# Loading x for a fused attention and gated-MLP kernel: all tiles by DMA transposes from the first issue, the second half of w_in on one queue

## The chip, the cores and the metric

The kernel runs on one core of a Trainium2 chip. The metric is the device time of one execution in microseconds (us). A profile's span, from the first to the last instruction, is about 1.7 us shorter than that time (before: 207.5 us of span, 209.19 us of time in the same execution). Times of the kernel before spread over about 1 us, and a finding at the end shows what may make most of that.

## The reference

```python
x = A_x                                             # [1, 2048, 512] bf16
g = sigmoid((x * gate_w).sum(-1, keepdims=True))
a = hedgehog_linear_attention(x, wqkv, w_phi, wo)   # 32 heads of 16
z = gelu(x @ w_in)                                  # [2048, 1376]
z1 = z[..., :688]
z2 = layernorm(z[..., 688:])
b = (z1 * (w_sp @ z2 + b_sp)) @ w_out
return g * a + (1 - g) * b
```

The argument touches only the first step: `z2 = x @ w_in[:, 688:]`, for which x must lie transposed in SBUF.

## The kernel before

x has 16 tiles of 128 rows. In the kernel before, tiles 0 to 3 come by plain loads (`xs`) and TensorE (PE) transposes them; tiles 4 to 7 come by one DMA transpose each, tiles 8 to 15 by two of four tiles. The second half of w_in, `w_z2`, comes in four pieces of 172 KB (one for each 128 rows of the contraction, `dt`), three on ScalarE's queue and one on SyncE's. PE runs warm-up matmuls while it waits for the first data. One extra column of `w_z2` holds the gate vector: `gate_T` puts it there through PE and VectorE, and the second half (`j = 1`) of each z2 tile needs it.

```python
nc.sync.dma_start(out=xs[:, 0, :], in_=x2[0:P, :])
load_z2w(nc.scalar, 0)                      # w_z2 piece 0
nc.sync.dma_start(out=xs[:, 1, :], in_=x2[P:2 * P, :])
load_z2w(nc.scalar, 1)
load_z2w(nc.sync, 2)
nc.scalar.dma_start(out=gaterow[0:NDT, :], in_=gate_w.rearrange(...))
load_z2w(nc.scalar, 3)
nc.sync.dma_start(out=xs[:, 2:4, :], in_=...)          # tiles 2 and 3
for h in range(2):
    nc.sync.dma_start(out=w_z1[:, 2 * h:2 * h + 2, :], in_=...)
for i in range(4, 8):
    nc.sync.dma_start_transpose(out=xT[:, :, i * P:(i + 1) * P], in_=x2[i * P:(i + 1) * P, :])
# ... (cut)

def z2_first_two():
    # ... (cut)
    warm_up(6)                              # 128x512 matmuls on constants
    warm_up(5, P)                           # 128x128
    x_T(0, 0, 1, ...)                       # PE transposes of tile 0, copy to xT
    x_T(0, 1, NDT, ..., on_act=True)
    warm_up(3, P)
    one(0, 0, 0)                            # tile 0, dt 0, half 0
    # ... (tiles 0 and 1 interleaved, gate_T among them, transposes of 2 and 3; cut)

with tc.manual_schedule(engines={PE, Activation}):
    z2_first_two()
    z2_tile(2)
    z2_tile(3)
    b_T()                                   # a tiny matmul; then z1 begins
    # ... (cut)
```

The softmax here doesn't subtract the row's maximum and nothing guards it: scores larger than these inputs give would overflow.

## Time and profile before

| | before |
|---|---|
| time, median of the first 3 runs | 208.36 us (208.36 to 209.25) |
| span of the profiled run | 207.5 us |
| PE busy | 203.6 us, 98% |
| start of z1 (just after `b_T`) | 11.35 us |

Two lines of the page of before: the busy time of PE, and the chain that ended last by engine.

```profile
PE 203.6 (98%) x1456; PEld 122.5 (59%) x1456; DVE 131.4 (63%) x282; ACT 75.4 (36%) x122; POOL 46.6 (22%) x78
...
PE 98%; DVE 0%; issue 0%
```

PE bounds the kernel. Its first microseconds are another matter. The next lines are the chain of waits of before in order of time (start, length in us, what; L226 is the warm-up, L284 a transpose of x, L195 a matmul of z2 or z1, L294 the gate, L299 `b_T`).

```profile
0.84 3.25 PE zp L226 x11
4.10 0.43 PE pq L284 x4
...
4.84 0.29 PE zp L195
...
6.06 0.57 PE zp L195 x2
6.63 0.01 PE pq L294
6.64 1.34 PE zp L195 x8
...
9.01 2.34 PE zp L195 x16
11.35 0.01 PE pq L299
11.35 14.03 PE zp L195 x96
```

Read the length of one matmul from them: 0.57/2 = 0.29 us at 6.06, 2.34/16 = 0.146 us from 9.01 on. The array clock doubles in between; the trace's record of the granted clock has its first entry, full speed, at 6.70 us. (Before its first entry this record counts as 1.00 in the views, so the "PEclk" column says nothing of the first microseconds; the length of the matmuls does.) From 9.01 us on PE never waits again.

The DMA engines in that stretch of before: each line has a window in us, its length, PE's busy time and instructions, the granted clock, the mean busy share of the 16 DMA engines and the GB/s that they moved. A share above 1 means that packets overlap within an engine.

```profile
4.00:5.00 1.00, 1.00 (x10) 1.00 1.04 329
5.00:6.00 1.00, 1.00 (x9) 1.00 1.05 374
6.00:7.00 1.00, 1.00 (x7) 1.00 1.09 344
7.00:8.00 1.00, 1.00 (x11) 1.00 1.18 331
```

A load's landing is the time at which its last bytes have arrived. By its DMA issues the plain loads of tiles 0 and 1 landed about 3 us after their issue, the pieces of w_in 3.1 to 3.9 us after theirs (tile, queue, number of loads, size of one, median us from issue to landing):

```profile
xs<-in_A_x_dram SPq DMA_DIRECT2D x2, 128.0 KB, 3.1
w_z<-in_B_w_in_dram ACTq DMA_DIRECT2D x3, 172.0 KB, 3.5
```

### The profile page before, as it was taken

The numbers are of one execution on the slowest core, as the hardware profiler recorded it, in microseconds if no ns is written. First come the engines' busy times: TensorE is split into PE (matmuls) and PEld (weight loads), VectorE is DVE, ScalarE is ACT, GpSimd is POOL, SyncE is SP. The second block draws the span as 40 slices with busy tenths as digits, with TensorE's granted clock in tenths as the row PEclk, the third lists the DMA queues.
The fourth block names the chain that finished last, engine by engine and source line by source line (L and its number), as shares of the span: only waits on it lengthen the run. The fifth ranks groups of instructions, "written<-read, shape, count | busy, mean of one in ns | idle before, by whom it ended". The sixth has DMA issues, their size and how long they took to land.

```text
span 207.5 us, 3776 instructions
## 1 busy us (share of the span) xinstructions
PE 203.6 (98%) x1456; PEld 122.5 (59%) x1456; DVE 131.4 (63%) x282; ACT 75.4 (36%) x122; POOL 46.6 (22%) x78
## 2 busy tenths in 40 slices
PE   8999999999999999999999999999999999999994
PEld 4666666765566555556565666555455555665642
DVE  2477786764977777879797788555466563633330
ACT  3665666666422232333323033222251126002322
POOL 7020202020542227243342422222204220200000
PEclk9999999999999999999999999999999999999999
DMA  6999999999922014971403236753564469253442
GB/s 189 263 187 202 242 290 218 267 284 179 290 38 43 0 38 89 254 179 33 92 18 71 50 41 115 144 106 70 108 160 89 76 114 182 56 104 65 132 89 77
DMA packets 88970, 27.20 MB, mean 131 GB/s; under 512 B 82968, under 2 KB 88952, under 8 KB 88952
## 3 DMA queue, kind: packets, MB, share of 16 engines
q1 hardware_dynamic: 86176, 24.37, 59.1%
q10 hardware_dynamic: 2744, 2.60, 4.3%
q8 instruction: 11, 0.18, 0.4%
q14 instruction: 7, 0.06, 0.1%
q0 software_dynamic: 32, 0.00, 0.0%
HBM read 4.41 MB, written 2.10 MB: 31 GB/s over the span
## 4 chain that ended last, share of the span: by engine, by line
PE 98%; DVE 0%; issue 0%
PE mm L457 36%; PE zp L195 18%; PE mm L366 13%; PE mm L496 8%; PE mm L494 7%; PE mm L406 7%; PE at L470 2%; PE kvacc L422 2%; PE zp L226 2%; PE mm L499 1%; PE pq L319 1%; PE pq L284 1%; DVE ob L506 0%; PE pq L305 0%; PE tp L284 0%
## 5 line engine op out<-in xcount | busy, mean ns | idle before, releaser
L457 PE MATMUL mm<-z2all,wspT 128*128 128x344 bf16 x512 | 79.9, 309 | 0.0
L457 PEld LDWEIGHTS <-wspT 128*128 128x128 bf16 x512 | 49.0, 98 | 25.7 <-issue 0.4
L195 PE MATMUL zp<-w_z,xT 128*128 128x344 bf16 (+1 forms) x256 | 40.6, 312 | 0.0
L370 ACT ACTIVATE eq<-mm 128x512 bf16<-128x512 f32 x32 | 17.4, 594 | 51.3 <-POOL eq L383 21.5
L374 DVE TENSOR_REDUCE zs<-eq 128x64 f32<-128x1024 bf16 x16 | 19.5, 1220 | 20.3 <-ACT eq L370 20.3
L195 PEld LDWEIGHTS <-xT 128*128 128x128 bf16 x256 | 24.7, 99 | 11.2
L462 DVE SCALAR_TENSOR_TENSOR ucat<-mm,bT,z1all 128x344 bf16<-128x344 f32 x32 | 17.4, 544 | 21.8 <-PE mm L457 21.8
L383 POOL TENSOR_TENSOR eq<-eq,ratio 128x512 bf16<-128x512 bf16 x16 | 16.9, 1058 | 50.2 <-DVE ratio L382 41.7
L370 ACT ACTIVATE ek<-mm 128x512 bf16<-128x512 f32 x32 | 17.3, 600 | 27.1 <-PE mm L366 27.1
L510 ACT ACTIVATE ob<-mm,g_inv 128x512 bf16<-128x512 f32 (+1 forms) x16 | 10.9, 681 | 32.8 <-PE mm L499 28.3
L374 DVE TENSOR_REDUCE zs<-ek 128x64 f32<-128x1024 bf16 x16 | 19.3, 1209 | 2.8 <-ACT ek L370 2.8
L496 PE MATMUL mm<-wspT,uT 128*128 128x512 bf16 (+2 forms) x85 | 20.1, 366 | 0.0
L366 PEld LDWEIGHTS <-xT 128*128 128x128 bf16 x128 | 12.2, 98 | 12.9 <-PE mm L499 0.8
L383 POOL TENSOR_TENSOR ek<-ek,ratio 128x512 bf16<-128x512 bf16 x16 | 16.9, 1059 | 2.0 <-DVE ratio L382 1.2
L494 PE MATMUL mm<-wspT,oT 128*128 128x512 bf16 (+2 forms) x68 | 16.6, 366 | 0.0
L366 PE MATMUL mm<-wq_p,xT 128*128 128x512 bf16 x64 | 16.4, 379 | 0.0
L406 PE MATMUL mm<-wv_sb,xT 128*128 128x512 bf16 x64 | 16.4, 379 | 0.0
L366 PE MATMUL mm<-wk_p,xT 128*128 128x512 bf16 x64 | 16.3, 379 | 0.0
L213 DVE BATCH_NORM_STATS2 bn<-z2all 128x6 f32<-128x344 bf16 x32 | 14.9, 502 | 0.0
L210 ACT ACTIVATE z2all<-zp 128x688 bf16<-128x688 f32 x16 | 11.8, 744 | 7.3 <-PE zp L195 6.8
L264 ACT ACTIVATE z1all<-zp 128x688 bf16<-128x688 f32 x16 | 11.9, 744 | 6.7 <-PE zp L195 6.7
L496 PEld LDWEIGHTS <-uT 128*128 128x128 bf16 x85 | 8.1, 98 | 9.2
(79 smaller groups left out, 150.9 us busy)
## 6 DMA issues: line engine op xcount, KB each, us to landing
out_dram<-ob ACTq DMA_DIRECT2D x15, 128.0 KB, 1.8
wspT<-in_B_w_out_dram SPq DMA_DIRECT2D x2, 640.0 KB, 5.6
w_z<-in_B_w_in_dram SPq DMA_DIRECT2D x2, 344.0 KB, 4.2
w_z<-in_B_w_in_dram ACTq DMA_DIRECT2D x3, 172.0 KB, 3.5
wv_sb<-in_A_wqkv_dram SPq DMA_DIRECT2D x1, 512.0 KB, 4.7
wspT<-in_A_wo_dram SPq DMA_DIRECT2D x1, 512.0 KB, 6.2
xs<-in_A_x_dram SPq DMA_DIRECT2D x2, 128.0 KB, 3.1
xs<-in_A_x_dram SPq DMA_DIRECT2D x1, 256.0 KB, 4.3
```

The source lines that it names most:

```text
L195: nc.tensor.matmul(zp[:, j, 0:n], lhsT=xT[:, dt, tt * P:(tt + 1) * P], rhs=wt[:, dt, j * HF:j * HF + n], start=(dt == 0), stop=(dt == NDT ...
L213: nc.vector.bn_stats(out=bn6[:, tt, j, :], in_=z2v[:, j, :])
L264: nc.scalar.activation(out=z1all[:, tt, :].rearrange("p (j n) -> p j n", j=2), in_=zp[:, :, 0:HF], func=AF.Gelu_apprx_tanh,)
L366: nc.tensor.matmul(ps[:, :], lhsT=xT[:, dt, tt * P:(tt + 1) * P], rhs=w[:, dt, :], start=(dt == 0), stop=(dt == NDT - 1))
L370: nc.scalar.activation(out=e[:, :, a, :], in_=ps[:, :].rearrange("p (h f) -> p h f", f=DH), func=AF.Exp, scale=1.0 - 2.0 * a)
L374: nc.vector.tensor_reduce(out=z[:].rearrange("p h a -> p (h a)"), in_=e[:].rearrange("p h a f -> p (h a) f"), axis=AX.X, op=ALU.add,)
L383: nc.gpsimd.tensor_tensor(out=e[:, :, 1, :], in0=e[:, :, 1, :], in1=ratio[:, :, None].to_broadcast([P, H, DH]), op=ALU.mult)
L406: nc.tensor.matmul(v_ps[:, :], lhsT=xT[:, dt, tt * P:(tt + 1) * P], rhs=wv_sb[:, dt, :], start=(dt == 0), stop=(dt == NDT - 1))
L457: nc.tensor.matmul(gp[:, 0:HF], lhsT=wspT[:, st, tt * P:(tt + 1) * P], rhs=z2all[:, st, j * HF:(j + 1) * HF], start=(st == 0), stop=(st == ...
L462: nc.vector.scalar_tensor_tensor(out=ucat[tt % NU][:, c0 + j * HF:c0 + (j + 1) * HF], in0=gp[:, 0:HF], scalar=bT[:, tt:tt + 1], in1=z1all[ ...
L494: nc.tensor.matmul(acc, lhsT=oT[:, g, :], rhs=wo_t[:, g, c0:c1], start=(g == 0), stop=False)
L496: nc.tensor.matmul(acc, lhsT=uT[:, i + ft, :], rhs=w_main[i][:, ft, c0:c1], start=False, stop=False)
```

## The change

The intent: no PE transposes, no copies, no `xs` buffer; x arrives transposed. Two two-tile DMA transposes are the first issues on SyncE's queue, and all four pieces of `w_z2` go to ScalarE's queue, so that nothing stands before the transposes.

```diff
+X_FIRST = [(0, 2), (2, 4)]
-    nc.sync.dma_start(out=xs[:, 0, :], in_=x2[0:P, :])
-    load_z2w(nc.scalar, 0)
-    nc.sync.dma_start(out=xs[:, 1, :], in_=x2[P:2 * P, :])
-    load_z2w(nc.scalar, 1)
-    load_z2w(nc.sync, 2)
+    for dt in range(2):
+        load_z2w(nc.scalar, dt)
     nc.scalar.dma_start(out=gaterow[0:NDT, :], ...)
-    load_z2w(nc.scalar, 3)
-    nc.sync.dma_start(out=xs[:, 2:4, :], ...)
+    for dt in range(2, NDT):
+        load_z2w(nc.scalar, dt)
+    for r0, r1 in X_FIRST:
+        nc.sync.dma_start_transpose(out=xT[:, :, r0 * P:r1 * P], in_=x2[r0 * P:r1 * P, :])
     # w_z1 loads unchanged
-    for i in range(4, 8):          # one tile each
+    for i in range(4, 8, 2):       # two tiles each
 ...
-    def z2_first_two():            # (cut)
+    def z2_first():
         warm_up(6)
-        warm_up(5, P)
+        warm_up(6, P)
-        ...                        # transposes and interleaved tiles 0 and 1 (cut)
+        for dt in range(NDT):
+            z_one(zp, 0, w_z2, FH + 1, dt, 0)
         gate_T()
+        for dt in range(NDT):
+            z_one(zp, 0, w_z2, FH + 1, dt, 1)
+        z2_out(0, zp)
 ...
-        z2_first_two()
+        z2_first()
+        z2_tile(1)
         z2_tile(2)
```

More of the change, by code (lines that the diff above doesn't have):

```diff
@@ L93 @@
     ident = early.tile([P, P], BF16, name="ident")
-    xs = early.tile([P, 4, D], BF16, name="xs")
     gaterow = early.tile([P, P], BF16, name="gaterow")
@@ L120, in load_z2w @@
         eng.dma_start(out=w_z2[:, dt, 0:FH], in_=w_in_v[:, dt, FH:F])
-    nc.sync.dma_start(out=xs[:, 0, :], in_=x2[0:P, :])
-    load_z2w(nc.scalar, 0)
-    nc.sync.dma_start(out=xs[:, 1, :], in_=x2[P:2 * P, :])
-    load_z2w(nc.scalar, 1)
-    load_z2w(nc.sync, 2)
+    for dt in range(2):
+        load_z2w(nc.scalar, dt)
     nc.scalar.dma_start(out=gaterow[0:NDT, :], in_=gate_w.rearrange("(dt p) -> dt p", p=P))
-    load_z2w(nc.scalar, 3)
-    nc.sync.dma_start(
-        out=xs[:, 2:4, :], in_=x2[2 * P:4 * P, :].rearrange("(i p) d -> p i d", p=P))
+    for dt in range(2, NDT):
+        load_z2w(nc.scalar, dt)
+    for r0, r1 in X_FIRST:
+        nc.sync.dma_start_transpose(out=xT[:, :, r0 * P:r1 * P], in_=x2[r0 * P:r1 * P, :])
     for h in range(2):
@@ L133 @@
             out=w_z1[:, 2 * h:2 * h + 2, :], in_=w_in_v[:, 2 * h:2 * h + 2, 0:FH])
-    for i in range(4, 8):
-        nc.sync.dma_start_transpose(out=xT[:, :, i * P:(i + 1) * P], in_=x2[i * P:(i + 1) * P, :])
+    for i in range(4, 8, 2):
+        nc.sync.dma_start_transpose(out=xT[:, :, i * P:(i + 2) * P], in_=x2[i * P:(i + 2) * P, :])
     for q in range(2, NCH):
@@ L217, in z2_tile @@
         z2_out(tt, z_mm(tt, w_z2, FH + 1))
-    def z2_first_two():
-        zps = [zp_tile() for _ in range(2)]
-        tp1 = psA.tile([P, 2, P], BF16, name="tp1", tag=next_turn("zp", 3))
-        turn["zp"] -= 1
+    def z2_first():
+        zp = zp_tile()
         def warm_up(n, w=CH):
@@ L226, in warm_up @@
                 nc.tensor.matmul(
-                    zps[0][:, 1, 0:w], lhsT=nc.const_aps.tensor(1.0, [P, P], BF16),
+                    zp[:, 1, 0:w], lhsT=nc.const_aps.tensor(1.0, [P, P], BF16),
                     rhs=nc.const_aps.tensor(1.0, [P, w], BF16), start=True, stop=True)
-        def one(tt, dt, j):
-            z_one(zps[tt], tt, w_z2, FH + 1, dt, j)
         warm_up(6)
-        warm_up(5, P)
-        x_T(0, 0, 1, pq_tile([P, 1, P], BF16)[:, :, :])
-        x_T(0, 1, NDT, pq_tile([P, 3, P], BF16)[:, :, :], on_act=True)
-        warm_up(3, P)
-        one(0, 0, 0)
-        x_T(1, 0, 2, tp1[:, :, :])
-        x_T(1, 2, NDT, pq_tile([P, 2, P], BF16)[:, :, :], on_act=True)
-        one(0, 1, 0)
-        warm_up(2, P)
-        one(1, 0, 0)
-        one(1, 1, 0)
-        gate_T()
-        one(0, 2, 0)
-        one(1, 2, 0)
-        for dt in range(2):
-            one(0, dt, 1)
-            one(1, dt, 1)
-        one(0, 2, 1)
-        one(1, 2, 1)
-        x_T(2, 0, NDT, pq_tile([P, NDT, P], BF16)[:, :, :])
-        one(0, 3, 0)
-        one(0, 3, 1)
-        z2_out(0, zps[0])
-        one(1, 3, 0)
-        one(1, 3, 1)
-        z2_out(1, zps[1])
-        x_T(3, 0, NDT, pq_tile([P, NDT, P], BF16)[:, :, :])
+        warm_up(6, P)
+        for dt in range(NDT):
+            z_one(zp, 0, w_z2, FH + 1, dt, 0)
+        gate_T()
+        for dt in range(NDT):
+            z_one(zp, 0, w_z2, FH + 1, dt, 1)
+        z2_out(0, zp)
     def z1_tile(tt):
@@ L280, in z2_norm @@
             )
-    def x_T(i, d0, d1, tp, on_act=False):
-        for dt in range(d0, d1):
-            nc.tensor.transpose(tp[:, dt - d0, :], xs[:, i, dt * P:(dt + 1) * P], ident[:, :])
-        dst = xT[:, d0:d1, i * P:(i + 1) * P]
-        if on_act:
-            nc.scalar.copy(out=dst, in_=tp)
-        else:
-            with tc.high_priority():
-                nc.vector.tensor_copy(out=dst, in_=tp)
     def gate_T():
```

## The prediction

> **What bounds it now.** TensorE. The page's first part has PE busy 203.6 of 207.5 us, and the chain of waits is 98% PE. But the chain's first 9 us are not all useful: 3.25 us of warm-up matmuls up to 4.09, four transposes of x, three more warm-ups, and the first real matmul at 4.84. Real matmuls last 0.29 us each until about 6.8 us and 0.146 us afterwards: the array clock doubles there. Tile 2 of z2 starts at 9.01 us; from then on each tile takes a steady 1.17 us and no DMA is ever waited for. So only the time at which tile 2 starts can move the total, microsecond for microsecond.
>
> **What the change removes.** 16 PE transposes: eight at 0.11 us cold for tiles 0 and 1 (0.85 us), eight at 0.055 us warm for tiles 2 and 3 (0.44 us); some 128-wide warm-ups; six copies on VectorE and ScalarE (0.23 to 0.48 us each); one ScalarE table load.
>
> **What it adds.** Two DMA transposes of two tiles at the very start, instead of plain loads that land 2.9 and 3.1 us after issue. By the DMA issues one-tile transposes hold the queue 1.26 us and four-tile ones 1.87 us, so I estimate 1.47 us for two tiles; landing came 1.6 to 4.4 us after the end of the issue. Tiles 0 and 1 then land at 0.81+1.47+2.4 = 4.7 us (4.2 to 5.7). All four w_in pieces now queue on ScalarE; the last lands near 6.3 us (3.9 us after an issue near 2.5): the bytes of the first 6 us are the same. The Trainium skill, "DMA: Bandwidth & Descriptors", section "Issuing engines are not separate DMA queues", says that another issuing engine saves issue time only; no run here shows it yet.
>
> **The start, costed.** Warm-ups end near 4.1 us; PE idles 0.6 us or more, does dt 0 and 1 of tile 0, waits for dt 2 and 3 to about 6.3, then about 0.4 us for the gate column (PE, VectorE copy 0.18, back), which the old order hid behind other matmuls. The Trainium skill, "TensorE: Matmul & The Clock Gate", Part 1, says that the clock rises only after a busy window of about 3.4 us, free-running. The trace agrees so far: full speed came about 6 us after the first warm-up. With holes between 4.1 and 7 us I expect the fast clock a window later, near 10 us: tile 0 ends near 8.1, tile 1 (8 matmuls at 0.29) near 10.3. Tile 2 starts 1.3 us later than before; in a lucky phase (fast from 6.8) 0.3 us earlier; in an unlucky one up to 3 us later.
>
> Tiles 4 to 7 take 2.9 us of queue instead of 5.1, but PE never waited for them, so that is worth nothing.
>
> **Prediction: 209.3 us, 80% range 207.8 to 211.2; faster by over 2% 0.02, within 2% 0.93, slower by over 2% 0.05.**
>
> **What would show it.** Right: first real matmul at 4.5 to 5.7 us, PE's idle before it put down to a DMA; 0.29 us matmuls beyond 7 us; tile 2 starting at 9.5 to 11 us; the rest of the chain unchanged (about 198 us after that start). Wrong in the step of arrival: x landing before 4.3 us or after 6. Wrong in the step of the clock: 0.146 us matmuls before 7 us in spite of holes.
>
> **What would make it wrong.** Transposes landing faster beside plain loads than later in the trace (a gain near 1 us); transposes slowed by the w_in loads, so that tile 0 comes after 6.5 us; a wait for w_z1 or tiles 4 to 7; a clock that drops back.

## The result

The changed kernel took 213.83 us, median of 4 runs (213.0 to 213.99); before took 208.36 us (208.31 to 209.25) beside it. The ratio is 1.0244, 95% interval 1.0207 to 1.0282: slower. A ratio here is the mean time of one kernel's fast runs over that of the other's fast runs of the same rounds, so it is not quite the ratio of the medians. Executions over 1.5% slower than the fastest of the same kernel are left out of the means. The span grew by 4.66 us, from 207.45 to 212.11. That is less than the 5.47 us between the medians: the profiled run of before, at 209.19 us, is one of its slower ones.

The busy time and the chain by engine of the changed kernel:

```profile
PE 203.3 (96%) x1418; PEld 121.3 (57%) x1436; DVE 130.4 (61%) x278; ACT 73.3 (35%) x119; POOL 46.4 (22%) x78
...
PE 94%; DMA 3%; DVE 1%; issue 1%; ACTq 0%
```

PE is busy for as long as before, but the chain now has DMA in it. Its start in order of time (L193 is now the matmul of z2 and z1, L257 the gate, L258 the copy of the gate column, L262 `b_T`, L120 the issue of a piece of w_in on ScalarE's queue):

```profile
2.36 0.36 ACTq L120
...
2.75 6.24 DMA w_z<-in_B_w_in_dram
...
9.03 0.44 PE zp L193
9.48 0.05 PE pq L257
...
9.55 0.18 DVE w_z L258
...
9.78 6.13 PE zp L193 x28
15.90 0.01 PE pq L262
15.91 14.03 PE zp L193 x96
```

The last piece of w_in took 6.24 us to land, at 8.99 us, where before it took 3.9. The four pieces together, by the DMA issues:

```profile
w_z<-in_B_w_in_dram ACTq DMA_DIRECT2D x4, 172.0 KB, 4.5
```

The 28 matmuls after it took 6.13 us, 0.22 us each on average, where 28 at 0.146 would take 4.1: the clock's record has full speed only from 13.62 us on. z1 starts at 15.91 us instead of 11.35, 4.56 us later, and that is the whole difference but for 0.1 us: from there to the end it is 196.2 us, against 196.1 in before (212.11 - 15.91 and 207.45 - 11.35).

PE's waits for DMA in the first 20 us of the changed kernel (total us, times, longest):

```profile
PE zp L193 <- DMA xT<-in_A_x_dram: 1.9, 1, 1.9
PE zp L193 <- DMA w_z<-in_B_w_in_dram: 1.6, 1, 1.6
```

The first wait ended at 6.14 us, when x landed (5.3 us after its issue at 0.81). The same windows as above, for the changed kernel:

```profile
4.00:5.00 1.00, 0.20 (x2) 1.00 1.20 187
5.00:6.00 1.00, 0.00 (x0) 1.00 1.12 201
6.00:7.00 1.00, 0.81 (x3) 1.00 1.25 193
7.00:8.00 1.00, 0.39 (x1) 1.00 1.21 150
```

The DMA engines are as busy as before and move 183 GB/s in the mean of the four instead of 345.

### The profile page after: what moved, and what is told of

It reads as the page before. It is cut to its first block, busy times and chain, and to the rows that moved or that the text cites. A ratio compares the mean times of both kernels' runs of the same rounds, so it can differ in the third digit from the quotient of the medians.

```text
span 212.1 us, 3709 instructions
## 1 busy us (share of the span) xinstructions
PE 203.3 (96%) x1418; PEld 121.3 (57%) x1436; DVE 130.4 (61%) x278; ACT 73.3 (35%) x119; POOL 46.4 (22%) x78
## 3 DMA queue, kind: packets, MB, share of 16 engines
HBM read 3.89 MB, written 2.10 MB: 28 GB/s over the span
## 4 chain that ended last, share of the span: by engine, by line
PE 94%; DMA 3%; DVE 1%; issue 1%; ACTq 0%
PE mm L421 35%; PE zp L193 19%; PE mm L330 13%; PE mm L460 8%; PE mm L370 7%; PE mm L458 6%; DMA w_z<-in_B_w_in_dram 3%; PE at L434 2%; PE kvacc L386 2%; PE mm L463 1%; PE pq L282 1%; DVE ident L114 0%; ACTq L120 0%; DVE ob L470 0%; PE pq L268 0%
## 5 line engine op out<-in xcount | busy, mean ns | idle before, releaser
L193 PE MATMUL zp<-w_z,xT 128*128 128x344 bf16 (+1 forms) x256 | 42.0, 321 | 3.9 <-DMA xT<-in_A_x_dram 1.9
L193 PEld LDWEIGHTS <-xT 128*128 128x128 bf16 x256 | 25.3, 101 | 15.5 <-DMA xT<-in_A_x_dram 2.2
L330 PEld LDWEIGHTS <-xT 128*128 128x128 bf16 x128 | 12.2, 98 | 13.0 <-PE mm L463 0.8
L208 ACT ACTIVATE z2all<-zp 128x688 bf16<-128x688 f32 x16 | 11.9, 743 | 14.5 <-PE zp L193 14.0
L458 PE MATMUL mm<-wspT,oT 128*128 128x512 bf16 (+2 forms) x62 | 15.6, 365 | 0.3
L237 ACT ACTIVATE z1all<-zp 128x688 bf16<-128x688 f32 x16 | 11.9, 743 | 6.7 <-PE zp L193 6.7
```

The source lines that it names most:

```text
L193: nc.tensor.matmul(zp[:, j, 0:n], lhsT=xT[:, dt, tt * P:(tt + 1) * P], rhs=wt[:, dt, j * HF:j * HF + n], start=(dt == 0), stop=(dt == NDT ...
L208: nc.scalar.activation(out=z2v, in_=zp[:, :, 0:HF], func=AF.Gelu_apprx_tanh)
L330: nc.tensor.matmul(ps[:, :], lhsT=xT[:, dt, tt * P:(tt + 1) * P], rhs=w[:, dt, :], start=(dt == 0), stop=(dt == NDT - 1))
L458: nc.tensor.matmul(acc, lhsT=oT[:, g, :], rhs=wo_t[:, g, c0:c1], start=(g == 0), stop=False)
```

## The experiments

The theory formed from the traces: the transposes and the plain pieces of w_in, in flight together from two queues, slow each other (MIXING). Its rivals: four pieces in a row on one queue make the last one late (QUEUE); a first two-tile transpose simply takes 5.3 us (LATENCY). Beside these, how much of the loss is the late clock (CLOCK)?

This table sums up the profiled run of each kernel. "x" and "last w" are the landings of tiles 0 and 1 and of the last piece of w_in (issue plus time to landing; a dash where x came by plain loads); "fast clock" is the start of full speed by the record of the granted clock, with a fall back to half noted; "rest" is span less start of z1. All times in us; the ratio is to before on the same chip, whose median there was 208.36 to 209.0. Each landing comes from one profiled run: with the same loads in the same order the last piece came at 9.0 and 9.4 us (changed and a_fill) and at 6.2 and 6.4 us (before and b_pairs_later), so differences below about 0.4 us say nothing.

| kernel | x | last w | fast clock | z1 starts | rest | median time | ratio |
|---|---|---|---|---|---|---|---|
| before | - | 6.2 | 6.70 | 11.35 | 196.1 | 208.36 | 1 |
| changed | 6.1 | 9.0 | 13.62 | 15.91 | 196.2 | 213.83 | 1.0244 |
| b_act_queue | - | 7.9 | 6.57 | 11.75 | 196.1 | 210.92 | 1.0106 |
| a_fill | 6.5 | 9.4 | 6.77 | 14.26 | 196.2 | 212.31 | 1.0173 |
| a_x_then_w | 4.8 | 9.0 | 4.25, half 7.66 to 14.49 | 16.34 | 196.3 | 214.34 | 1.0272 |
| a_w_then_x | 6.9 | 5.6 | 12.52 | 14.75 | 196.3 | 212.09 | 1.0156 |
| b_act_queue2 | - | 7.7 | 4.18 | 11.88 | 196.2 | 209.77 | 1.0050 |
| a_split | 5.7 | 5.9 | 3.55, half 6.97 to 10.38 | 12.78 | 196.2 | 211.04 | 1.0088 |
| a_T23_late | 5.5 | 7.8 | 4.84, half 8.26 to 11.67 | 14.26 | 196.2 | 212.76 | 1.0187 |
| a_wx_fill | 7.0 | 5.5 | 5.28 | 11.88 | 196.3 | 209.82 | 1.0040 |
| a_z1_first | 5.7 | 8.6 | 4.62, half 8.03 to 14.86 | 16.32 | 196.2 | 214.43 | 1.0267 |
| a_split_fill | 5.8 | 6.1 | 4.82 | 10.70 | 196.2 | 208.90 | 0.9998 |
| b_T23 | - | 6.7 | 6.49 | 10.97 | 196.1 | 208.68 | 0.9980 |
| b_pairs_later | - | 6.4 | 4.25 | 10.53 | 196.2 | 208.79 | 1.0001 |
| a_T01_only | 5.4 | 7.5 | 4.42, half 7.83 to 11.25 | 14.36 | 196.2 | 212.98 | 1.0192 |
| a_wz1_ahead | 9.6 | 9.7 | 16.11 | 17.91 | 196.2 | 215.66 | 1.0322 |
| b_T23_pairs | - | 6.2 | 4.07 | 10.26 | 196.2 | 208.71 | 0.9995 |

The rest is 196.1 to 196.3 us in all seventeen. Whatever these edits did, they did it before z1 starts. Names with b_ are edits of before, with a_ of the changed kernel.

### b_act_queue: all of w_in on ScalarE, in the kernel before

```diff
-    load_z2w(nc.sync, 2)
+    load_z2w(nc.scalar, 2)
```

> The kernel before, with the third piece of w_in moved from the SyncE queue to the ScalarE queue and nothing else: one part of the change alone. Theory MIXING (the DMA transposes of x and the plain loads of w_in, in flight together on the same DMA engines, slow each other): there is no transpose in this start, so the last piece lands by about 7 us and the time stays within 0.5 us of before. Rival QUEUE (four pieces in a row on one queue make the last one late): the last piece lands near 9 us as in the changed kernel and the time rises by 2 us or more.

Measured: 210.92 us (209.54 to 212.02), ratio 1.0106 (1.0057 to 1.0155). The expectation of MIXING, within 0.5 us, was missed. QUEUE had the time (2.26 us more by the medians) but not the landing (7.9 us, not near 9). The experiment had a fault too. The loads share eight completion semaphores in turn, and the last piece had become the ninth, so its issue waited for the first piece to land (3.89 us instead of 2.36), and ScalarE's copies of x behind it were late. The profiled run was the fastest of the four; of what made the slowest 2.5 us longer no trace exists, so it stays open.

### a_fill: the changed kernel, PE's holes filled

```diff
         warm_up(6, P)
+        warm_up(4)
         for dt in range(NDT):
+            if dt == 3:
+                warm_up(5)
             z_one(zp, 0, w_z2, FH + 1, dt, 0)
```

> The changed kernel with nine more 512-wide warm-up matmuls in the two holes in which PE waits for x and for the last piece of w_in, so that PE stays busy from 0.85 to 9 us. The loads are untouched. Theory CLOCK (of the 5 us lost, about half is the arrival of data, the other half the fast clock that comes a window or two late because of the holes): matmuls run at 0.146 us from about 7 us on, z1 starts near 13.7 us instead of 15.9, and the time falls by about 2.2 us against the changed kernel, to about 211.6. Rival (arrival alone): no change, 213.8, or a little worse from fillers in the way.

Measured: 212.31 us (211.69 to 212.69), ratio 1.0173 (1.0149 to 1.0198). The chain of waits of this run:

```profile
2.72 6.63 DMA w_z<-in_B_w_in_dram
...
10.00 4.26 PE zp L193 x28
```

The 28 matmuls take 4.26 us instead of 6.13, although the data came 0.36 us later than in the run of the changed kernel. So about 1.9 us of the loss was the clock, as CLOCK had it; the time fell by 1.5 us, not by the 2.2 expected, for the late data took some of it back. The arrival of data and the gate hole are the rest.

### a_x_then_w: one queue, transposes first

```diff
-    for dt in range(2):
-        load_z2w(nc.scalar, dt)
     nc.scalar.dma_start(out=gaterow[0:NDT, :], ...)
-    for dt in range(2, NDT):
-        load_z2w(nc.scalar, dt)
     for r0, r1 in X_FIRST:
         nc.sync.dma_start_transpose(...)
+    for dt in range(NDT):
+        load_z2w(nc.sync, dt)
```

> The changed kernel with all four pieces of w_in issued on the SyncE queue after the two transposes: the same bytes on one queue, in order, so that transposes and plain loads hardly overlap. MIXING: the first transpose lands at 4.3 to 5.0 us (not 6.1), the last piece of w_in at about 7.5 us (not 9.0), and the time falls by 0.5 to 2 us against the changed kernel, although w_in is issued later. Rival LATENCY (a first two-tile transpose takes about 5.3 us by itself): x again at 6.1 us, w_in later than 9 us, the time 214 or more.

Measured: 214.34 us (213.94 to 214.59), ratio 1.0272 (1.0252 to 1.0291). x landed at 4.8 us (4.0 us after its issue), as MIXING expected and not at 6.1: LATENCY falls. The time did not fall, though. The last piece came at 9.0 us, 1.5 us later than I expected, and PE stood idle from 4.2 to 6.8 us, so the clock, fast at 4.25, fell back to half from 7.66 to 14.49 us. Two windows of this run matter later:

```profile
3.00:4.00 1.00, 1.00 (x8) 1.00 1.02 210
...
7.00:8.00 1.00, 0.37 (x2) 0.83 0.72 198
```

In the first only transposes moved, and the busy engines carried 210 GB/s; in the second only plain loads moved (the second transpose had landed at 5.6 us), and they were slow as well.

### a_w_then_x: one queue, w_in first

```diff
-    for dt in range(2):
-        load_z2w(nc.scalar, dt)
     nc.scalar.dma_start(out=gaterow[0:NDT, :], ...)
-    for dt in range(2, NDT):
-        load_z2w(nc.scalar, dt)
+    for dt in range(NDT):
+        load_z2w(nc.sync, dt)
     for r0, r1 in X_FIRST:
         nc.sync.dma_start_transpose(...)
```

> The changed kernel with all four pieces of w_in issued on the SyncE queue ahead of the two transposes: again one queue, in order. MIXING: w_in all landed by about 4.7 us, the first transpose at 5.8 to 6.5 us, after which no load is waited for: z2 tile 0 runs straight through, the time falls by 1.5 to 3 us against the changed kernel (about 211 to 212.3), still above before because of the cold clock. LATENCY: x lands at 2.5+5.3 = 7.8 us or later, the time within 1 us of the changed kernel.

Measured: 212.09 us (211.35 to 212.88), ratio 1.0156 (1.0114 to 1.0197). w_in was there at 5.6 us (expected 4.7), x at 6.9 (expected 5.8 to 6.5), 4.2 us after its issue. Both were a little late, but nothing was waited for after x, and the time lies where MIXING put it. The slow clock until 12.52 us is most of what it lost to before.

### b_act_queue2: the same question as b_act_queue, without the fault

```diff
-    load_z2w(nc.sync, 2)
-    nc.scalar.dma_start(out=gaterow[0:NDT, :], ...)
+    load_z2w(nc.scalar, 2)
+    nc.gpsimd.dma_start(out=gaterow[0:NDT, :], ...)
```

> The run b_act_queue had a fault as an experiment: only eight completion semaphores go round the queued loads, and the last piece of w_in had become the ninth, so ScalarE waited for the first piece before it issued it, and its copies of x came late. Here the tiny gate load goes to the GpSimd queue, so that all four pieces of w_in issue on ScalarE without a wait. QUEUE: the last piece lands near 9 us and the time rises by 2 us or more. MIXING: the last piece lands by about 6.5 us, first real matmul at 4.8 to 5.1 us, the time within 0.7 us of before; if the time is above that although the loads are early, it is the clock again.

Measured: 209.77 us (209.33 to 210.87, the three fast runs; the fourth, 212.84, was slow), ratio 1.0050 (1.0009 to 1.0092). The last piece landed at 7.7 us, between the two expectations: the fourth place on a queue costs 1.5 us against before (6.2) with no transpose beside it, but not the 2.8 us of the changed kernel. The edit also let the first w_z1 load go out at 2.24 us instead of 3.98, so "place" here includes that load beside the last piece. A new fault came in: the gate load on GpSimd's queue took 4.8 us, and PE waited 1.2 us for it. It is the gate, not w_in, that set this start.

### a_split: transposes kept, one piece back on SyncE ahead of them

```diff
-    for dt in range(2, NDT):
-        load_z2w(nc.scalar, dt)
+    load_z2w(nc.sync, 2)
+    load_z2w(nc.scalar, 3)
```

> The changed kernel with the third piece of w_in back on the SyncE queue, ahead of the transposes: the transposes alone, with the old division of w_in. QUEUE: the last piece lands by about 7 us and the time falls by 1.5 us or more. MIXING: the same bytes and transposes are in flight together, so the last piece still lands after 8 us and x at 6 to 6.8 us; the time stays within 1 us of the changed kernel's 213.8.

Measured: 211.04 us (209.11 to 211.95), ratio 1.0088 (1.0031 to 1.0146). MIXING, as I had put it, failed here: the last piece landed at 5.9 us and x at 5.7, with the second transpose in flight until 6.8 us, and the time fell by 2.8 us. QUEUE had foretold that. Moving one load of 172 KB recovers more than half of the loss. The windows of this run show that the engines moved 303 and 273 GB/s with both kinds in flight, and then its other half:

```profile
4.00:5.00 1.00, 0.00 (x0) 1.00 1.26 303
5.00:6.00 1.00, 0.23 (x2) 1.00 1.18 273
6.00:7.00 1.00, 0.70 (x7) 0.98 1.09 336
7.00:8.00 1.00, 1.00 (x5) 0.50 1.05 369
8.00:9.00 1.00, 1.00 (x6) 0.50 1.21 260
...
10.00:11.00 1.00, 1.00 (x8) 0.81 0.93 205
```

The granted clock falls to 0.50 at 6.97 us and comes back at 10.38, 3.41 us later. PE had been idle from 4.0 to 5.8 us.

### a_T23_late: the second transpose behind the w_z1 loads

```diff
-    for r0, r1 in X_FIRST:
+    for r0, r1 in X_FIRST[0:1]:
         nc.sync.dma_start_transpose(...)
     # w_z1 loads
+    for r0, r1 in X_FIRST[1:2]:
+        nc.sync.dma_start_transpose(...)
```

> The changed kernel with the second transpose (tiles 2 and 3) issued behind the two w_z1 loads. MIXING: half of the transposed bytes are out of the way of w_in, so the last piece lands about 1.5 us earlier (7 to 7.8 us) and the first transpose at 5 to 5.8; the time falls by 0.5 to 2 us, unless tile 2 then waits for its x. QUEUE: no change in the last piece's landing (9 us).

Measured: 212.76 us (212.17 to 213.01), ratio 1.0187 (1.0161 to 1.0214). The last piece landed at 7.8 us, 1.2 us earlier than in the changed kernel, still fourth on its queue, and x at 5.5. That is the direction of MIXING; QUEUE expected no change.

### a_wx_fill: w_in first, gate column early, holes filled

The edit is a_w_then_x with:

```diff
         warm_up(6, P)
+        gate_T()
+        warm_up(6)
         for dt in range(NDT):
             z_one(zp, 0, w_z2, FH + 1, dt, 0)
-        gate_T()
```

> The run a_w_then_x (no overlap of w_in and transposes) with the gate column made before x lands, and six more 512-wide warm-ups, so that PE is busy until x lands near 6.9 us and its clock is fast from then on. If arrival, clock and the hole at the gate column are the whole loss, z1 starts at 11.6 to 11.9 us (before: 11.35) and the time is 208.6 to 209.4, within 0.6 us of before. If something else in the change costs time, it stays above 210.

Measured: 209.82 us (209.56 to 209.91), ratio 1.0040 (1.0019 to 1.0062). z1 starts at 11.88 us as expected (11.6 to 11.9), the time is 0.8 us above before, a little more than foretold. Its chain:

```profile
2.68 4.30 DMA xT<-in_A_x_dram
...
7.02 4.85 PE zp L191 x32
```

32 matmuls in 4.85 us are 0.15 us each, without a hole. 2.3 us of the 212.09 are gone with the data arriving as late as in a_w_then_x. The later start (0.53 us) leaves about 0.3 us of the 0.8 unexplained, within the spread of before; no larger loss is hidden in the change.

### a_z1_first: four pieces on ScalarE, another load ahead of the transposes

```diff
+    nc.sync.dma_start(out=w_z1[:, 0:1, :], in_=w_in_v[:, 0:1, 0:FH])
     for r0, r1 in X_FIRST:
         nc.sync.dma_start_transpose(...)
-    for h in range(2):
-        nc.sync.dma_start(out=w_z1[:, 2 * h:2 * h + 2, :], ...)
+    nc.sync.dma_start(out=w_z1[:, 1:4, :], in_=w_in_v[:, 1:4, 0:FH])
```

> The run a_split changed two things at once: one piece less on ScalarE's queue, and 172 KB of plain load ahead of the transposes, which start half a microsecond later. Here all four pieces stay on ScalarE, and the 172 KB ahead of the transposes are a piece of w_z1, which nobody needs yet. OVERLAP (what costs is the time in which transposes and pieces of w_in are in flight together; a short head start of the plain loads shortens it): first transpose at 5.7 to 6.3 us, the last piece of w_in at 6.3 to 7.7 us, time 211 to 212.3. QUEUE (fourth place on one queue): last piece at 8.5 us or later, time 213 or more.

Measured: 214.43 us (213.39 to 216.13), ratio 1.0267 (1.0223 to 1.0312). x landed at 5.7 us, as in a_split, but the last piece at 8.6: OVERLAP, in this form, missed, and QUEUE hit. A head start for the plain loads is not enough; the fourth piece is what comes late. In the trace's packet records of this run the packets of 1376 bytes (w_in, from 6.5 us on w_z1 too) take 122 to 204 ns on average in the half microseconds from 6 to 8 us, while the second transpose is in flight, against 59 ns in most of before.

### a_split_fill: a_split without its holes

The edit is a_split with:

```diff
         warm_up(6, P)
+        warm_up(2)
+        gate_T()
+        warm_up(2)
         ...
-        gate_T()
```

> The run a_split with its PE hole filled (four more 512-wide warm-ups) and the gate column made before x lands. Data arrives at 5.8 us as there. If arrival, clock and gate hole are the whole story, z1 starts at 10.8 to 11.4 us (before 11.35, a_split 12.78) and the time is 208.2 to 209, equal to before or up to 0.3% faster, and the runs lie closer together than those of a_split (209.1 to 212.0). If the PE transposes of before were worth something else, or the holes are not the cause of a_split's loss, it stays near 211.

Measured: 208.90 us (208.44 to 209.29, 6 runs), ratio 0.9998 (0.9972 to 1.0023). The transposes, well placed, with PE kept busy, are as good as before and need no PE transpose. z1 starts at 10.70 us (expected 10.8 to 11.4), and the runs spread over 0.9 us where a_split's spread over 2.8.

```profile
1.27 4.51 DMA xT<-in_A_x_dram
...
5.83 4.85 PE zp L193 x32
```

### b_T23: before, with only tiles 2 and 3 by a DMA transpose

```diff
-    nc.sync.dma_start(out=xs[:, 2:4, :], ...)
+    nc.sync.dma_start_transpose(out=xT[:, :, 2 * P:4 * P], in_=x2[2 * P:4 * P, :])
...
-        x_T(2, 0, NDT, pq_tile([P, NDT, P], BF16)[:, :, :])
...
-        x_T(3, 0, NDT, pq_tile([P, NDT, P], BF16)[:, :, :])
```

> The kernel before with only tiles 2 and 3 through a two-tile DMA transpose, in the place of their plain load, and their eight PE transposes gone: a small part of the change alone. The eight transposes are 0.44 us of PE in the chain. OVERLAP: the last piece of w_in, in flight with this transpose, lands at 6.5 to 7.5 us instead of 6.3, still before PE needs it near 8; the time is 0 to 0.5 us under before. If a transpose in flight with w_in hurts as much as in the changed kernel, the last piece comes after 8.5 us and the time rises by 0.5 to 2 us.

Measured: 208.68 us (207.99 to 208.98, 6 runs), ratio 0.9980 (0.9955 to 1.0004). The last piece landed at 6.7 us, before PE needed it. A gain of 0.2% as foretold, but the interval includes none.

### b_pairs_later: before, with tiles 4 to 7 in pairs

```diff
-    for i in range(4, 8):
+    for i in range(4, 8, 2):       # two tiles each
```

> The kernel before with tiles 4 to 7 in two transposes of two tiles instead of four of one: the part of the change that comes after the start. PE never waited for these tiles, so the time stays within 0.4 us of before; the two transposes hold the queue about 3 us instead of 5.2.

Measured: 208.79 us (208.50 to 210.04), ratio 1.0001 (0.9968 to 1.0034). This part is worth nothing that can be seen; the two transposes held the queue for 3.85 us, not 3.

### a_T01_only: the second transpose replaced by a plain load

The edit puts the plain load of tiles 2 and 3, and their PE transposes, back into the changed kernel:

```diff
-    for r0, r1 in X_FIRST:
+    for r0, r1 in X_FIRST[0:1]:
         nc.sync.dma_start_transpose(...)
+    nc.sync.dma_start(out=xs[:, 2:4, :], ...)
```

> The changed kernel with tiles 2 and 3 loaded plainly in the same place of the queue and transposed on PE, as before; the first transpose and all four pieces of w_in on ScalarE stay. COLLISION (the fourth piece is late because it is in flight together with the second transpose): the last piece lands at 6.5 to 7.9 us instead of 9.0, the time 211.5 to 213. PLACE (the fourth place on ScalarE's queue does it, whatever runs beside it): 8.5 us or later, time 213.5 or more.

Measured: 212.98 us (212.27 to 213.62), ratio 1.0192 (1.0160 to 1.0223). The same bytes at the same place of the queue, but plain:

```profile
4.00:5.00 1.00, 0.21 (x2) 1.00 1.17 253
5.00:6.00 1.00, 0.47 (x2) 1.00 1.08 311
6.00:7.00 1.00, 0.31 (x1) 1.00 1.00 352
7.00:8.00 1.00, 0.31 (x2) 0.92 1.05 384
```

The engines move 325 GB/s in the mean instead of 183, and the last piece, still fourth, lands at 7.5 us. COLLISION holds, PLACE alone does not: its 8.5 us did not come.

### a_wz1_ahead: both transposes behind the w_z1 loads

```diff
+    # w_z1 loads moved up here
     for r0, r1 in X_FIRST:
         nc.sync.dma_start_transpose(...)
-    # w_z1 loads
```

> The changed kernel with both w_z1 loads (688 KB) issued ahead of the two transposes: w_in and w_z1, all plain, run side by side first, the transposes come after. COLLISION: the last piece of w_in, still fourth on ScalarE, lands at 5.8 to 7.2 us; x comes last, at 7 to 8.5 us, and sets the start, so the time is 212.5 to 214. PLACE: last piece at 8.5 us or later.

Measured: 215.66 us (215.54 to 215.86), ratio 1.0322 (1.0295 to 1.0348). The expectation of COLLISION missed: the last piece came at 9.7 us and x at 9.6, and PLACE's "8.5 us or later" was met. The 688 KB of w_z1 took their share first, so the last two pieces were still in flight when the transposes came: the collision was moved, not removed, and the run does not tell the two theories apart. But it shows a fast and a slow stretch within one trace, plain loads alone in the first line, both kinds after:

```profile
4.00:5.00 1.00, 0.20 (x2) 1.00 1.07 392
6.00:7.00 1.00, 0.00 (x0) 1.00 1.18 182
7.00:8.00 1.00, 0.00 (x0) 1.00 1.26 162
```

### b_T23_pairs: the harmless parts together

The edit is b_T23 and b_pairs_later.

> The kernel before with the two parts of the change that did no harm: tiles 2 and 3, and tiles 4 to 7, in two-tile DMA transposes; tiles 0 and 1 and the queues of w_in as before. Eight PE transposes (0.44 us) are gone from the chain. Expected ratio to before 0.997 to 0.999, about half a microsecond faster, hardly outside the noise that the clock's start makes; if b_T23's gain was chance, 1.000.

Measured: 208.71 us (208.20 to 209.35, 6 runs), ratio 0.9995 (0.9971 to 1.0020). No gain that can be told from none. No version here is shown to beat before; a_split_fill, b_T23, b_pairs_later and this one cannot be told from it.

## Why the prediction was wrong

The prediction was 209.3 us, 207.8 to 211.2, "same". The time was 213.83 us, slower by 2.4%. Point by point:

- **What bounds the kernel, and that only the start counts: right.** The rest after z1's start is 196.1 to 196.3 us in all seventeen kernels.
- **The cost of the transpose itself: right.** I estimated 1.47 us of issue and a landing 3.9 us after it; undisturbed (a_x_then_w) it was 1.33 and 4.0 us.
- **The step that failed: the arrival of data, "Tiles 0 and 1 then land at 0.81+1.47+2.4 = 4.7 us" and "the last lands near 6.3 us ...: the bytes of the first 6 us are the same".** They landed at 6.1 and 8.99 us. The same bytes did not take the same time: 512 KB of them had become transposes, and from 4 to 8 us the engines moved 183 GB/s where plain loads moved 345. The prediction had named "transposes slowed by the w_in loads" as a risk, but gave it no cost, and it was the last piece of w_in, not x, that set the start. The size of the two causes of the late last piece: with no transposes beside it, the fourth place on ScalarE's queue put it at 7.7 us (b_act_queue2) instead of 6.2; taking the second transpose away brought it from 9.0 to 7.5 (a_T01_only), putting it behind the w_z1 loads to 7.8 (a_T23_late). So about 1.5 us is the place and about 1.2 to 1.5 us the second transpose. The transposes without the place do no harm to w_in: with one piece moved to SyncE's queue, ahead of both transposes, the last landed at 5.9 us (a_split). It took both to make 9.0.
- **The clock: right in kind, too small in size.** I expected full speed "near 10 us"; it came at 13.62, about two windows after the 6.70 of before, since the holes lasted until 9.8 us.
- **The gate hole, about 0.4 us: right.** The chain shows 9.48 to 9.78, 0.30 us.

The sum of the 4.56 us by which z1 starts later: if everything after the last piece had run at full speed and without the gate hole, 29 matmuls at 0.146 us from 9.03 would have ended at 13.26 us. That is 1.91 us after 11.35: the arrival, against what before did with its time. The other 15.91 - 13.26 = 2.65 us are the slow clock (about 2.3) and the gate hole (about 0.3). a_fill measured the clock's part by itself: its 28 matmuls were 1.87 us faster. And the two together, arrival and holes mended (a_split_fill), bring the ratio to 0.9998.

The Trainium skill, "DMA: Bandwidth & Descriptors", section "Issuing engines are not separate DMA queues", says that all queues end on the same 16 engines and interleave, and that another issuing engine saves only issue time. The interleaving is seen here; the conclusion that I drew, that the division between queues is of no matter, is not what the runs show: a_split against the changed kernel moves one load to the other queue and is 2.8 us faster. The same head start given to another load, with four pieces left on ScalarE, gained nothing (a_z1_first).

What stays open: why the engines moved only half as much in the changed kernel. That both kinds were in flight is not enough, for a_split moved 303 and 273 GB/s so. Part of it is that transposes are slower by themselves: 210 GB/s in a_x_then_w, from 3 to 4 us. In the packet records 78 of the 183 GB/s are packets of 256 bytes, the size that transposes have in that stretch; an estimate from the two rates, 210 and 345, would be 271 GB/s for this mixture. The rest, down to 183, is not explained, and plain loads without a transpose can be slow too (198 GB/s in a_x_then_w, from 7 to 8 us). The packets of 1376 bytes, which are pieces of w_in and w_z1, lasted 103 to 210 ns on average in the half microseconds from 4 to 8 us in the changed kernel, against 59 to 78 ns in before, but the trace does not say what they waited for.

## What to carry to other kernels

Bytes are not the cost of a load: plan the first microseconds by which transfers are in flight together, and issue the plain loads that the first matmuls need early enough that none of them is left for last beside DMA transposes. Keeping the two kinds apart is no cure by itself: a_x_then_w did that and lost as much as the changed kernel (1.0272 and 1.0244), while a_split mixed them and lost least of the versions without fillers (1.0088). Read a start from the last operand to land, then give PE something to do until it lands, since in a_split a hole of 1.8 us cost a further 3.4 us at half clock. A small move of one load (a_split), four fillers and an earlier gate column turned a loss of 2.4% into none.

## What the Trainium skill lacked or had wrong

- "DMA: Bandwidth & Descriptors", "Rules for kernel authors": it says that a transpose next to ordinary DMAs needs nothing. That row is about wrong results, and every experiment here gave correct ones. For speed it can matter: 183 GB/s with both in flight against 345 GB/s with plain loads (4 to 8 us, changed kernel and before), and 182 against 392 GB/s within one trace (a_wz1_ahead), though a_split moved 303 and 273 GB/s with both. The page has no number for the two together.
- The same page, "Issuing engines are not separate DMA queues": that spreading loads over queues only saves issue time leaves out the place that a load gets in its queue. One 172 KB load moved to the head of the other queue: 213.83 us against 211.04 (ratios to before 1.0244 and 1.0088).
- "TensorE: Matmul & The Clock Gate", "HAM oscillation — how this bites in real kernels": the rule there is no idle gap above about 3.4 us. The window of 3.41 us, from the page's Part 1, agrees with the trace (the half-speed stretches of a_split and a_x_then_w last 3.41 and 6.83 us), but the clock fell after a gap of 1.8 us (a_split, PE busy for 38% of the window that ended at 6.97 us) and after gaps of which no more than 0.8 us each lay in the window (a_T23_late, 32% busy, at 8.26 us), and held through a gap of 1.2 us (b_act_queue2, 65% busy). The busy share of the window fits these runs, a limit of 3.4 us on one gap does not. For the rise, a window busy for 79% sufficed (a_split, at 3.55 us) and one busy for 74% did not (a_fill, whose clock rose one window later at 6.77), but one busy for 80% did not either (a_wz1_ahead, at 12.70 us, a window before its rise at 16.11), so near 80% the busy time of the trace does not decide it.
- The same page says that the window runs free. The runs agree: with the same warm-ups, full speed came at 4.1 to 4.3 us in two of the profiled runs of before's family (b_pairs_later, b_T23_pairs) and at 6.5 to 6.7 in others (before, b_T23), and z1's start moves by 0.8 us with it (10.53 in b_pairs_later against 11.35 in before). This is nearly as large as the spread of before's times, 208.3 to 209.3 us, though only one run of each kernel has a trace. The page calls the whole ramp less than 1% of a typical kernel; this shift alone is 0.4% here, and twice the gain that b_T23 sought.
- No page that I read says that loads of one program share a small set of completion semaphores in turn: in b_act_queue the last piece had become the ninth load and its issue waited until 3.89 us instead of 2.36, just after the first piece had landed (3.87). This comes from how the program was built, and one has to look for it when loads are moved.
